# Loading the first weight in partition halves over two queues, with a new instruction order, in a fused FFT filter and GELU MLP kernel

## The chip, the cores and the metric

The kernel runs on one core of a Trainium2 chip. The metric is device time in microseconds (us) of one execution. The profile is one execution taken by the hardware profiler; its span is the time between its first and last instruction. Five engines run their own instruction streams and wait for each other by semaphores: PE (matmuls), VectorE (DVE), ScalarE (ACT), GpSimd (POOL) and SyncE (SP). A DMA can be issued from the queue of SyncE, ScalarE or GpSimd.

## The reference

```
xn  = layernorm(x)                       # x: 2048 x 640, bf16, no scale or shift
A   = irfft2(rfft2(xn) * (w_r + 1j*w_i)) # filter over both axes; w: 2048 x 321
B   = gelu(xn @ w1 + b1) @ w2 + b2       # w1: 640 x 1536, w2: 1536 x 640, tanh gelu
out = x + A + B                          # bf16
```

## The kernel before

The 2048 rows are cut into 16 chunks of 128 rows (chunk c holds rows 16p + c). All work is written as operations of a small scheduler class; each has a number in the order of its creation. The string `ORDER` lists all numbers, each with the letter of its engine (s, p, a, d, g) and its buffer slots, and so fixes the order on every engine by hand; `sync` only adds the waits. The times written at the loads (`at`) and the durations in the operations were for choosing the order: they do not reach the program.

*Loads.* SyncE's queue issues the chunks 0 and 1 of x singly (called x0 and x1 here, 160 KB each), then the five row blocks of W1 (block j holds rows 128j to 128j+127, 128 partitions x 3072 bytes, 384 KB each), then chunks 2 and 3 of x in one transfer (here x2, 320 KB), the table G (gtab, 512 KB), the other chunks in pairs, the bias b2, W2 in three parts (640 KB each), smaller tables, the filter weights (Wf, transfers of 16 partitions with runs of 642 bytes), and later a few more. ScalarE's queue issues one load, b1 (3 KB). `load` keeps the loads of one queue in their order.

*Layer norm, per chunk.* DVE computes statistics (`bn_stats`, two halves, line 478; `bn_aggr`, line 480). For chunk 0 ScalarE takes the square root (line 484) and DVE the reciprocal; then ScalarE loads the table for gelu (line 485). For the other chunks DVE adds eps (line 488) and GpSimd raises to -0.5 (line 489). DVE writes the normalised chunk (line 507).

*Transposes.* xnT holds the chunks with columns on partitions. Chunks 0 to 5 are transposed by PE (line 525) and copied by DVE and ScalarE (lines 394, 395); chunks 6 to 15 by DMA (line 516).

*Forward transform.* For a pair of chunks DVE folds the normalised rows (line 537, two operations, and line 541, four), the "T operations" of the pair; PE multiplies with gtab (ten matmuls a pair), and the result is copied to XV. When all eight pairs are there, PE goes on with etab, mtab and ntab (the filter and its way back), SyncE transposes the results by DMA, and PE ends with getab and htab.

*MLP.* The first layer of chunks 0 and 1 is made of 60 steps of two 128-wide matmuls: for each of six pairs of 128 hidden columns (b), chunk (t) and W1 block (j) one step, number 241 + 12b + 5t + j. A step waits for its block of W1, and the five blocks of one sum are taken in order. The remaining chunks follow in blocks of two and then four chunks (256 and 512 wide), gelu with bias b1col on ScalarE (lines 581, 599). The second layer (W2 times gT) fills PE between the steps of the transform; for some chunks it is done early and kept (line 759).

Before the first real work PE runs 47 matmuls on zeros (`warm`). All matmuls but the transposes have line 383, a helper.

Of the kernel before, what the change touches and what calls it, by code (L numbers as in the profile page):

```python
# [9 lines left out]
ACT = mybir.ActivationFunctionType  # L10
# [4 lines left out]
F = 1536  # L15
# [3 lines left out]
NFC = 12  # L19
# [277 lines left out]
def bass_parallel_sum__spectral_gfnet__dense_activation_gelu__prompt_kernel(  # L297
# [15 lines left out]
    w1v = B_w1.rearrange("(c p) f -> p c f", p=128)  # L313
# [5 lines left out]
    with ExitStack() as es:  # L319
# [131 lines left out]
        for ri, wsrc in enumerate((A_w_r, A_w_i)):  # L451
            for half in range(4):
# [4 lines left out]
                else:  # L457
# [14 lines left out]
        for c0, n in [(0, 1), (1, 1)] + [(c, 2) for c in range(2, 16, 2)]:  # L472
            pr = 100 - c0 / 2
            B_mv, B_ve, B_r = Buf("mv"), Buf("ve"), Buf("r")
            for c in range(c0, c0 + n):
                B_st = Buf("st")
                for h in range(2):
                    st_ops.append(K.op([("dve", 0.393)], pr, lambda e, _, c=c, h=h: e.bn_stats(stats[:, c, 6 * h:6 * h + 6], view(X, c * D + H2 * h, [[1, H2]])),  # L478
                         reads=[B_x[c]], writes=[B_st], hard=[first] if len(st_ops) == 2 else []))
# [12 lines left out]
        for pair in range(8):  # L492
            xn, x1, xf = Buf(f"xn{pair}", p_xn), Buf(f"xe{pair}", p_x1), Buf(f"xf{pair}", p_xf)

# [8 lines left out]
            for n in range(2):  # L503
# [15 lines left out]
                for j0, j1, engs in ((0, 3, ["dve"]), (3, 5, ["act"])) if c < 2 else ((0, 5, ["dve", "act"]),):  # L519
# [8 lines left out]
                    if j0 and not c:  # L528
# [280 lines left out]
```

## Time and profile before

| | us |
|---|---|
| median of 3 runs (151.99 to 152.57) | 152.36 |
| the profiled execution | 152.23 |
| its span | 150.4 |
| PE busy | 144.0 (96%) |
| DVE busy | 108.0 (72%) |
| ScalarE busy | 75.9 (50%) |
| GpSimd busy | 22.0 (15%) |

The granted clock of TensorE was 1.0 in all slices. Matmuls are pipelined and their ends are modelled, so a line's length covers a little of its neighbour; the start times and the idle times in front are what to go by. "SPq" and "ACTq" are the queues' own issuing instructions.

### The profile page before, as it was taken

How to read it: one execution, taken by the hardware profiler on the slowest of the kernel's cores; microseconds unless marked ns; L12 is line 12 of the kernel's file. 1: busy time of each engine (PE TensorE's matmuls, PEld its weight loads, DVE VectorE, ACT ScalarE, POOL GpSimd, SP SyncE). 2: the span in 40 equal slices, each digit the busy share in tenths (PEclk: the TensorE clock that was granted, in tenths of full speed). 3: DMA queues.
4: the chain of work that ended last, by engine and by line, in shares of the span. 5: the costliest groups of instructions: out<-in, count | busy, mean ns of one | idle time of the engine just before them, and what ended most of it. 6: DMA issues, size and time to landing. Idle time of an engine off the chain costs nothing.

```text
span 150.4 us, 4033 instructions
## 1 busy us (share of the span) xinstructions
PE 144.0 (96%) x1726; PEld 90.4 (60%) x1726; DVE 108.0 (72%) x236; ACT 75.9 (50%) x124; POOL 22.0 (15%) x35
## 2 busy tenths in 40 slices
PE   7779999999989999999999999999999999999993
PEld 7669997565555645445545545445666565665662
DVE  2739999989973559775989989720499859666622
ACT  3514994566978768788594552141765040042000
POOL 2102031112400012000000000000000292380330
PEclk9999999999999999999999999999999999999999
DMA  4999997889778928702620621896000366679093
GB/s 133 308 383 404 348 395 141 150 127 111 141 159 150 191 27 251 275 1 57 124 57 10 127 48 31 104 221 124 17 0 0 44 82 97 87 132 209 12 127 93
DMA packets 28499, 20.68 MB, mean 137 GB/s; under 512 B 18881, under 2 KB 25793, under 8 KB 28482
## 3 DMA queue, kind: packets, MB, share of 16 engines
q1 hardware_dynamic: 25888, 15.51, 42.9%
q0 software_dynamic: 2592, 4.92, 16.8%
q8 instruction: 13, 0.21, 0.6%
q14 instruction: 4, 0.03, 0.1%
q10 hardware_dynamic: 2, 0.00, 0.0%
HBM read 13.54 MB, written 5.24 MB: 125 GB/s over the span
## 4 chain that ended last, share of the span: by engine, by line
PE 80%; DMA 10%; DVE 6%; SPq 1%; issue 1%; ACT 1%; ACTq 0%
PE ps L383 79%; DMA W<-in_B_w_dram 4%; DMA xnT<-T 3%; DMA XV<-T 2%; DVE T L541 1%; DVE stats L478 1%; SPq L375 1%; PE ps L525 1%; DVE T L537 1%; DVE T L507 1%; DVE T L395 1%; DVE X L759 1%; ACT T L394 1%; SPq L691 0%; DVE mv L480 0%
## 5 line engine op out<-in xcount | busy, mean ns | idle before, releaser
L383 PE MATMUL ps<-xnT,W 128*128 128x512 bf16 (+2 forms) x360 | 58.4, 309 | 2.5 <-DMA W<-in_B_w_dram 1.9
L383 PE MATMUL ps<-W,gT 128*128 128x512 bf16 (+3 forms) x396 | 58.1, 295 | 0.0
L383 PEld LDWEIGHTS ps<-W,gT 128*128 128x128 bf16 x396 | 30.2, 98 | 22.9 <-issue 2.2
L383 PEld LDWEIGHTS ps<-xnT,W 128*128 128x128 bf16 x360 | 31.8, 114 | 19.8 <-DMA W<-in_B_w_dram 2.2
L599 ACT ACTIVATE gT<-ps,b1col 128x512 bf16<-128x512 f32 (+1 forms) x48 | 29.0, 637 | 10.6 <-PE ps L383 10.5
L775 POOL DMA_DIRECT2D out_dram<-W x14 | 12.6, 1079 | 74.0 <-DVE W L768 74.0
L394 ACT ACTIVATE Wf<-ps 128x960 bf16<-128x960 f32 (+1 forms) x10 | 8.2, 862 | 17.4 <-PE ps L383 17.4
L478 DVE BATCH_NORM_STATS2 stats<-X 128x6 f32<-128x320 bf16 x32 | 14.1, 478 | 2.1 <-DMA X<-in_A_x_dram 2.1
L666 DVE TENSOR_TENSOR T<-Y,Wf 128x1288 bf16<-128x1288 bf16 x16 | 12.6, 820 | 0.0
L394 ACT ACTIVATE XV<-ps 128x1280 bf16<-128x1280 f32 (+2 forms) x9 | 9.9, 1118 | 4.2 <-PE ps L383 4.2
L489 POOL TENSOR_TENSOR rstd<-ve,mhalf 128x2 f32<-128x2 f32 (+1 forms) x8 | 6.5, 814 | 31.6 <-DVE ve L488 31.6
L395 DVE CAST Xb<-ps 128x960 bf16<-128x960 f32 (+1 forms) x5 | 5.9, 1181 | 6.1 <-PE ps L383 6.1
L394 ACT ACTIVATE Xb<-ps 128x960 bf16<-128x960 f32 (+1 forms) x7 | 7.6, 1108 | 4.9 <-PE ps L383 4.9
L722 DVE TENSOR_TENSOR Wf<-Wf 128x960 bf16<-128x960 bf16 (+1 forms) x12 | 6.8, 599 | 2.8 <-ACT Wf L394 2.6
L394 ACT ACTIVATE T<-ps 128x512 bf16<-128x512 f32 (+1 forms) x12 | 4.6, 437 | 8.0 <-DMA XV<-T 5.2
L541 DVE TENSOR_TENSOR T<-T 128x512 bf16<-128x512 bf16 (+1 forms) x32 | 8.6, 315 | 0.1
L395 DVE CAST Y<-ps 128x644 bf16<-128x644 f32 x7 | 5.8, 828 | 3.7 <-PE ps L383 3.6
L768 DVE TENSOR_TENSOR W<-ps,b2bc 128x640 bf16<-128x640 f32 x6 | 4.9, 821 | 4.8 <-PE ps L383 4.8
L507 DVE TENSOR_SCALAR T<-X,mv,rstd 128x640 bf16<-128x640 bf16 x16 | 6.8, 438 | 1.7 <-issue 1.0
L394 ACT ACTIVATE Y<-ps 128x644 bf16<-128x644 f32 x9 | 6.3, 709 | 3.5 <-PE ps L383 3.5
L759 DVE TENSOR_TENSOR X<-ps,b2bc 128x640 f32<-128x640 f32 x7 | 5.7, 819 | 3.2 <-PE ps L383 3.2
L383 PE MATMUL ps<-getab,XV 32*128 32x160 bf16 (+1 forms) x128 | 7.5, 242 | 0.0
(52 smaller groups left out, 127.0 us busy)
## 6 DMA issues: line engine op xcount, KB each, us to landing
out_dram<-in_A_x_dram POOLq DMA_DIRECT2D x4, 640.0 KB, 7.1
X<-in_A_x_dram SPq DMA_DIRECT2D x7, 320.0 KB, 8.1
out_dram<-W POOLq DMA_DIRECT2D x14, 160.0 KB, 4.2
W<-in_B_w_dram SPq DMA_DIRECT2D x5, 384.0 KB, 6.6
W<-in_B_w_dram SPq DMA_DIRECT2D x3, 640.0 KB, 12.6
Wf<-in_A_w_r_dram SPq DMA_DIRECT2D x7, 160.5 KB, 3.9
Wf<-in_A_w_i_dram SPq DMA_DIRECT2D x7, 160.5 KB, 3.4
gtab<-c_G SPq DMA_DIRECT2D x1, 512.0 KB, 7.9
```

The source lines that it names most:

```text
L383: ins = e.matmul(o_, lhsT=lw, rhs=rh, start=st, stop=sp_, skip_group_check=True)
L394: return e.activation(dst(), src(), ACT.Copy, scale=scale)
L395: return e.tensor_copy(dst(), src())
L478: st_ops.append(K.op([("dve", 0.393)], pr, lambda e, _, c=c, h=h: e.bn_stats(stats[:, c, 6 * h:6 * h + 6], view(X, c * D + H2 * h, [[1, H2 ...
L489: K.op([("pool", 0.75)], 400 + pr, lambda e, _, a=a, b=b: e.tensor_tensor(out=rstd[:, a:b], in0=ve[:, a:b], in1=mhalf[:, a:b], op=ALU.pow) ...
L507: o = K.op([("dve", 0.356)], pr, lambda e, _, c=c, n=n, xnv=xnv: e.tensor_scalar(out=xnv(n, 0, [[1, D]]), in0=view(X, c * D, [[1, D]]), sc ...
L541: ring_ops.append(K.op([("dve", 0.333 if w == 128 else 0.136)], pr, lambda e, _, op=op, x1v=x1v, xfv=xfv, o_=o_, o0=o0, o1=o1, w=w: e.tens ...
L599: K.op([("act", act_us(128 * nt, 1) + 0.02)], pr + PRIO["gelu"], lambda e, _, c0=c0, nt=nt, fc=fc, hps=hps: e.activation(gT[:, fc, 128 * c ...
L666: filt_ops.append(K.op([("dve", 0.738)], pr, lambda e, _, k=k, Y=Y, TB=TB, pair=pair: e.tensor_tensor(out=view(TT, TB.slot * 8 * KP + k * ...
L722: K.op([("dve", 0.068 + n / 6)], pr + 2, lambda e, _, k=k, op=op, yo=yo, y2=y2, n=n: e.tensor_tensor(out=view(Wf, Y2 + y2.slot * 3 * D + ( ...
L759: kept_ops.append(K.op([("dve", 0.735)], 30, lambda e, _, kps=kps, xo=xo: e.tensor_tensor(out=xo, in0=psb(kps.slot, [[1, D]]), in1=b2bc[:] ...
L775: last.append(K.op([("pool", 0.9)], 450, lambda e, _, c=c, os_=os_: e.dma_start(ov[:, c, :], view(W1, OST + os_.slot * D, [[1, D]]), accum ...
```

## The change

Each block of W1 is loaded as two transfers of 64 partitions x 3072 bytes (192 KB): partitions 0 to 63 from ScalarE's queue, partitions 64 to 127 from SyncE's. The two halves share one semaphore. ScalarE's first half waits for the identity matrix that GpSimd makes (so that it is issued behind it); the other four follow it. x2 is issued behind the third half on SyncE, ahead of blocks 3 and 4. The operations get new numbers, five more from there on: a first-layer step is now 246 + 12b + 5t + j, the transposes of chunks 1, 2 and 3 are 133 and 135, 147, and 150, and the T operations of the first pair are 139 to 142.

The order on all engines is new. On PE, all six steps with block 0 now stand in front of the first with block 1, and 50 of the 60 steps in front of the transposes of chunks 2 and 3 (before, 54 steps and the gtab matmuls of pair 0); 8 of the 47 warm matmuls stand behind the first transposes, and the b1 matmuls ahead of them. On DVE, the four T operations of pair 0 now stand behind the statistics of chunks 2 and 3 instead of in front. On ScalarE, the gelu table load stands directly behind the square root instead of behind the first xnT copy. On GpSimd the identity comes first.

`hard` entries only hold the order search to a sequence on one engine (the table load in front of the copies, GpSimd's powers behind the loads queued there); they add no wait.

```diff
 ORDER = """
-9s 2a 1d 7g 0d 4g 8p:4 3g 11a 10s 6g 12s 13s 14s 15s 55d 54d 16s 17s 56d 60d 57a 18s 59d 121d:1 19s 125p:3 61d 20s 122p:1 124p:4 52p:3 62d 21s 123d 126a 63d 58a 22s 64g 301p:7
-277p:4 302p 23s 289p:2 253p:0 278p 265p:1 24s 127d 279p 290p 291p 53a 266p 25s 241p:6 133d:0 128p:5 130p:3 303p 26s 129d 242p 131a 254p 267p 132d 280p 27s 268p 282p 283p 134d:1
-284p 28s 285p 243p 136d 258p 281p 29s 304p 135d 286p 137d 294p 306p 30s 287a 244p 305p 270p 65d 307p 288a 31s 255p 295p 68d 292p 308p 32s 296p 309p 69d 297p 310p 66d 33s 139p:3 70d
+9s 2a 0d 3g 8p:7 11a 10s 4g 5g 12a 13s 14a 15s 16a 17s 19a 18s 60d 21a 59d 20s 1d 22s 61d 65d 62a 23s 63a 64d 126d:1 57p:2 24s 66d 25s 129p:1 127p:6 67d 26s 130p:0 131a 68d 128d
+69g 58a 27s 246p:6 258p:7 270p:5 28s 282p:4 294p:0 306p:1 132d 271p 29s 307p 283p 259p 138d:0 133p:2 30s 135p:3 295p 134d 247p 31s 136a 296p 284p 137d 248p 260p 32s 311p 74d 263p
+299p 251p 33s 252p 70d 275p 312p 272p 71d 34s 264p 287p 300p 301p 73d 35s 265p 308p 302p 72d 309p 75d 36s 266p 261p 76d 276p 142d:1 277p 77g 141d 288p 273p 297p 139d 278p 262p 267p
...
 """
...
-        for j, at in enumerate((4.6, 5.75, 6.9, 8.05, 9.2)):
-            load(W1[:, F * j:F * j + F], w1v[:, j, :], B_w1s[j], 393216, prio=next(pr), at=at)
-        load_x(2, 2, next(pr), at=10.1)
-        load(gtab[:], const["G"], B_g, 524288, prio=next(pr), at=11.4)
+        for j, at in enumerate((5.4, 6.4, 7.5, 9.5, 10.6)):
+            if j == 3:
+                load_x(2, 2, next(pr), at=8.4)
+            for q, p0 in (("act", 0), ("sp", 64)):
+                load(part(W1, p0, 64, F * j, [[1, F]]), w1v[p0:p0 + 64, j, :], B_w1s[j], 196608, q=q, prio=next(pr) if q == "sp" else 408 - j, at=at, reads=[] if q == "sp" else [B_id], group=f"w1_{j}")
+        load(gtab[:], const["G"], B_g, 524288, prio=next(pr), at=11.8)
...
-        K.op([("act", 0.2)], 200, lambda e, _: e.activation(b1col[:], psb(B_b1ps.slot, [[1, NFC]]), ACT.Copy), reads=[B_b1ps], writes=[B_b1c])
+        tob1 = K.op([("act", 0.2)], 200, lambda e, _: e.activation(b1col[:], psb(B_b1ps.slot, [[1, NFC]]), ACT.Copy), reads=[B_b1ps], writes=[B_b1c])
...
-                K.op([("act", 1.3)], 410, lambda e, _: e.preload_act_table(ACT.Gelu_apprx_tanh), reads=[B_ve], writes=[Buf("table2")])
+                table2 = K.op([("act", 1.3)], 410, lambda e, _: e.preload_act_table(ACT.Gelu_apprx_tanh), reads=[B_ve], writes=[Buf("table2")])
...
-                 reads=[B_ve, B_mh], writes=[B_r] + B_rs[a:b])
-
+                 reads=[B_ve, B_mh], writes=[B_r] + B_rs[a:b], hard=list(queued["pool"]))
+
+        tob1.hard.append(table2)
...
-                         reads=[tps], writes=[B_xnT[c]])
+                         reads=[tps], writes=[B_xnT[c]], hard=[table2] if not c and engs == ["act"] else [])
```

More of the change, by code (lines that the diff above doesn't have):

```diff
@@ L257 @@
-138p 67d 34s 246p 71d 269p 140a 256p 74d 72g 259p 271p 260p 77d 257p 261p 298p 272p 5g 247p 141d:0 293p 311a 273p 144d 142p:5 73d 145p:4 143a 262p 245p 146d 248p 274p 312a 249p
-250p 84d 325p:4 252a 90d 337p:5 276a 331p:7 82d 251a 326p 76d 332p 300a 340p:3 147d:0 275a 338p 148d 346p:6 299a 85d 347p 327a 343p:1 81d 348a 313p:2 75d 83d 314p 333a 78d 86d 341p
-101d 339a 322p:6 87d 263a 323p 98d 328p:7 315a 79d 97d 587p:4 80g 342a 108d 319p:2 264a 151d:0 88g 344p 324a 156d:0 329p 320p 150d 330a 588p 152d 159d 149d 316p:3 89d 317p 589p
@@ L260 @@
-171d:1 318a 173d 590p 321a 99d 176d:0 174s 334p:6 175d 157p:2 335p 93d 591p 336a 91d 172s 180d:1 92d 592p 158a 117d 604p:6 345a 105d 605p 35s 100d 178d 606p 177d 36s 179d 160p:0
-94d 37s 607p 114d 161a 95d 593d 608p 38s 96g 609p 162d:0 154p:0 610d 153p 181p:3 155a 182p 186d:1 349p:6 102d 184d 163d 373p:7 185s 183a 109d 350p 165d:1 103d 164d 374p 104g 166d
-39s 382p:4 167d 375a 106d 187s 168p:1 116d 351a 379p:5 189d:0 188d 380p 197d:0 169p 113d 358p:7 198s 170a 118d 193d:1 190d 352p:6 115d 110d 119d 199d 383p 40s 381a 120g 191d 192d
@@ L263 @@
-359p 384a 200s 107d 353p 202d:0 111d 194p:0 201d 112g 354a 195p 225d:1 361p:5 41s 196a 203d:0 205d 355p:4 42s 204d 206d 223d 356p 360a 228d:0 224s 362p 227d 207p:1 363a 210d:0 208p
-394p:6 232d:0 43s 209a 230d 231d 397p:5 212d 211s 229d 395p 357a 215d:0 234p:1 396a 233p 214d 44s 391p:7 218d:0 236a 213s 219d 392p 217d 216d 235a 400p:6 393a 221p:0 45s 220p 398p
-46s 222a 406p:4 226s 407p 399a 457p:0,0 47s 385p:5 458d 459a 48s 386p 49s 747d 460p:0,1 387a 408a 401p 462d 461a 367p:5 368p 478p:0 439p:4 479d:0 480a:1 440p 402a 475p:0 237g
@@ L269 @@
-527a 624p 450a 533d:0 513p:0 625p 514a:2 515d:1 626p 530d:1 516p:0 627p 517d 518a 640p:4 757d 521s 628p 472p:0,1 534d 522s 529d 641p 473a 642p 532d:0 474a 519s 643p 629d 644p 531d
-547p:0 520s 535d:1 645p 549d:1 548a:0 659p:6 536d 550p:0 660p 552d 551a 661p 553d:1 537p:0 662p 557d:0 539a:1 663p 646d 538a:2 664p 554d 540p:0 676p:4 541a 542d 677p 665d 546s 678p
-679p 558d 680p 545s 556d:0 681p 559d:1 555d 695p:6 560d 543s 696p 682d 697p 51s 561p:0 544s 712p:4 562d:0 563a:1 698p 564p:0 699p 565a 713p 566a 568s 700p 454p:0 701d 567s 714p
@@ L272 @@
-433p:7 715p 570s 434p 716p 435a 569s 442p:6 443p 427p:7 455p 428p 456a 717p 429a 669p:0 718d 444a 451p:6 670d:0 671a 421p:4 422p 673d:0 597p:0 672d 423a 675d:0 452p 598d:1 599a
-436p:7 453a 437p 674d 571p:0 438a 600d:0 614p:4 601d 572a:0 578p:6 602d:1 573a 579p 603d 580p 575d:0 683p:0 630p:2 684d:7 615p 616p 574d 685g 631d:0 611p:0 617p 612d:2 581p 702p:2
-618p 703d:5 619p 704g 620p 633p:0 621d:4 632g 577d:1 650p:4 576d 634a:1 622g 651p 635a 582p 613g 583p 637d:0 652p 636d 594p:2 584p 595d:7 653p 654p 585d:1 655p 639d:1 586g 686p:6
@@ new lines @@
+69g 58a 27s 246p:6 258p:7 270p:5 28s 282p:4 294p:0 306p:1 132d 271p 29s 307p 283p 259p 138d:0 133p:2 30s 135p:3 295p 134d 247p 31s 136a 296p 284p 137d 248p 260p 32s 311p 74d 263p
+299p 251p 33s 252p 70d 275p 312p 272p 71d 34s 264p 287p 300p 301p 73d 35s 265p 308p 302p 72d 309p 75d 36s 266p 261p 76d 276p 142d:1 277p 77g 141d 288p 273p 297p 139d 278p 262p 267p
+140d 289p 7g 290p 146d:0 269a 285p 286p 37s 249p 149d 291p 268a 250p 253p 147p:2 293a 38s 150p:7 79d 292a 279p 274p 148d 298p 151a 310p 313p 303p 153d:0 314p 315p 281a 254p 152d
@@ new lines @@
+255p 345p:7 316a 81d 333p:4 280a 334p 87d 317a 346p 78d 351p:5 335a 352p 156d:0 257a 143p:1 80d 82d 144p 347a 342p:4 90d 256a 343p 157d 321p:7 353a 155d 83d 336p:6 89d 344a 322p
+154d 145a 337p 86d 348p:5 324p:4 84d 98d 85g 349p 323a 113d 325p 158p:1 338a 88d 91d 159p 161d:0 326a 330p:7 164d 160a 327p:6 92d 121d 331p 93g 339p:4 122d 340p 114d 328p 332a
+165p:3 123d 350a 176d:1 162p:2 341a 318p:7 97d 177s 319p 329a 111d 592p:4 320a 167d:0 593p 305a 168d 39s 304a 110d 609p:6 166a 112d 610p 170d:0 178d 163a 611p 99d 94d 179s 95d 594p
@@ new lines @@
+115d 169d 595p 172d 40s 116d 119d 612p 117g 96d 41s 171d 613p 180d:0 173p:0 42s 105d 614p 215d:0 596p 615d 216s 597p 181d 174p 100d 360p:7 598d 101g 43s 361p 217d 6g 357p:4 103d
+218s 362a 185d:1 189d:1 358p 175a 191d 372p:5 106d 190s 182d 387p:7 359a 183d 184d 373p 193d:0 192s 186p:0 194d 187p 354p:4 118d 188a 196d:1 197d 44s 355p 198d 120d 388p 195d 45s
+356a 124d 369p:6 219d:0 125g 389a 107d 102d 370p 220d 374a 200p:1 199p 104d 228d:0 363p:4 201a 108d 230d 109g 384p:5 223d:0 231s 222d 224d 221d 378p:7 371a 204d:1 226p:0 202d 229s
@@ new lines @@
+225p 207d:0 364p 227a 206d 379p 209d:1 46s 375p:6 211d 208d 365a 210d 47s 376p 233d:0 380a 385p 48s 232d 212p:0 386a 213p 205s 234d:0 432p:7 237d 214a 236d 441p:5 235d 49s 433p
+377a 238p:0 203s 239p 426p:4 240d 241a 442p 50s 462p:0,0 443a 51s 453p:6 52s 464d 463a 427p 53s 465p:0,1 428a 54s 414p:5 467a 466d 415p 454p 434a 752d 480p:0 417p:4 481d:0 482a:1
+418p 416a 483p:0 390p:7 484a 485d 242g 391p 487d:0 468p:0,0 392a 243g 486d 419a 408p:7 490d:1 469a 244g 411p:4 491d 245g 470a 412p 489d:1 409p 488d 402p:5 493d:0 413a 492d 403p
@@ new lines @@
+455a 504p:0 423p:4 506a:0 505d:1 424p 404a 494p:0 425a 393p:5 495d:2 496a:1 429p:6 410a 497p:0 430p 499d 498a 450p:4 431a 502s 507p:0 394p 508d 509a 399p:6 503s 515d:1 471p:0,0
+514d 501s 396p:7 472d 473a 451p 55s 400p 395a 510d:0 500s 474p:0,1 452a 517d:0 456p:4 476d 475a 397p 444p:5 511d 398a 528p:0 513d:1 457p 530a:1 512d 459p:7 516d 529a:0 460p 458a
+518p:0 401a 445p 519d:1 405p:4 520a:2 406p 446a 531p:0 420p:6 532d 533a 421p 461a 538d:1 521p:0 422a 447p:7 539d 407a 435p:6 522d 523a 438p:5 535d:0 524s 477p:0,0 534d 439p 527s
@@ new lines @@
+478a 479d 448p 436p 440a 541d:1 552p:0 526s 536d:0 437a 366p:5 553d:1 554a:0 367p 525s 537d 449a 555p:0 540d 381p:4 556d 557a 645p:6 368a 563d:1 542p:0 382p 544d:0 543a:2 646p 383a
+559d:0 647p 545p:0 562d 648p 547a 558d 649p 546a 550s 628p:4 561d:0 564d:1 629p 560d 650p 551s 565d 630p 651d 631p 56s 632p 548s 681p:6 566p:0 549s 633p 568d:0 567a:1 682p 634d
+569p:0 683p 571d 570a 664p:4 575s 665p 684p 685p 572s 666p 686p 574s 667p 687d 668p 573s 669p 717p:6 670d 718p 762d 719p 720p 721p 722p 583p:4 723d 638p:0 700p:6 639d:1 640a 701p
@@ new lines @@
+584p 641d:0 576p:0 642d 585p 577a:0 578d 702p 644d:0 703p 643d 602p:0 580d:0 579d 704p 603a:1 604d 586p 705p 581d:1 674p:0 706d 582d 587p 676d:0 675a 619p:6 588p 606d:0 589p 599p:2
+590d:0 620p 671p:0 605d 655p:4 600d:4 656p 621p 672d:2 601g 652p:2 657p 653d:3 658p 608d:1 654g 659p 607d 622p 591g 660p 678d:0 661p 677d 616p:0 635p:2 662d:6 623p 617d:5 624p 625p
+636d:7 727p:4 618g 728p 680d:0 663g 710p:0 626d:4 637g 691p:6 712a:1 711d 673g 692p 693p 679d 627g 694p 713d:0 707p:2 714d 695p 696p 708d:3 697p 729p 709g 698d:5 730p 716d:1 699g
@@ L278 @@
+736p:6 715d 731p 737p 688p:0 732p 689d:0 733p 738p 734d:2 739p 735g 724p:2 763p:4 725d:7 764p 740p 726g 741p 742p 765p 690g 743d:1 745p:0 744g 753p:6 747a:1 754p 746a 766p 755p
+748d:0 749d 772p:5 756p 750d:0 767p 751d 768p 757p 769p 758p 770d:4 759p 771s 773p 774p 760d:3 775p 776p 777p 781p:4 778p 782p 783p 761s 779d 784p 785p 786p 780s 787p 788d 789s
 """
```

6 lines of the change are left out of this document (removed).

## The prediction

> **What bounds the kernel now.** The page first: PE is busy for 144.0 of 150.4 us, so the time is PE's fixed work plus PE's gaps. The table of slices gives PE, VectorE and the DMA engines:
>
> ```profile
> PE   7779999999989999999999999999999999999993
> ...
> DVE  2739999989973559775989989720499859666622
> ...
> DMA  4999997889778928702620621896000366679093
> ```
>
> PE has one weak place, the first three slices (0 to 11 us); DVE is full from 11 to 41 us. PE's own timeline shows the gaps (start, length, engine, what, idle before it):
>
> ```profile
> 5.27 0.45 PE L525 MATMUL ps<-ident,T 128*128 128x128 bf16 x5
> 5.65 0.56 PE L383 MATMUL ps<-ident,gT 1*128 1x1 bf16 x12
> 6.20 0.41 PE L383 MATMUL ps<-xnT,W 128*128 128x128 bf16 x4
> 8.34 0.75 PE L383 MATMUL ps<-xnT,W 128*128 128x128 bf16 x10 [1.73 <-DMA W<-in_B_w_dram]
> 9.29 0.75 PE L383 MATMUL ps<-xnT,W 128*128 128x128 bf16 x10 [0.20 <-DMA W<-in_B_w_dram]
> ...
> 42.72 1.92 PE L383 MATMUL ps<-xnT,W 128*128 128x512 bf16 x8 [0.55 <-DMA xnT<-T]
> ...
> 98.16 0.52 PE L383 MATMUL ps<-Z,ntab 32*32 32x320 bf16 x32 [0.30 <-ACT T L394]
> ```
>
> After the first transposes PE stands still for 1.73 + 0.20 + 0.55 + 0.30 = 2.78 us. That is all that an earlier start and a better order can win. DVE's timeline shows the partner that limits PE from 12 us on:
>
> ```profile
> 11.04 1.03 DVE L541 TENSOR_TENSOR T<-T 128x512 bf16<-128x512 bf16 x4
> 12.05 1.67 DVE L478 BATCH_NORM_STATS2 stats<-X 128x6 f32<-128x320 bf16 x4
> ...
> 42.75 0.45 DVE L507 TENSOR_SCALAR T<-X,mv,rstd 128x640 bf16<-128x640 bf16 x1 [0.96 <-issue]
> ...
> 45.46 1.03 DVE L541 TENSOR_TENSOR T<-T 128x512 bf16<-128x512 bf16 x4
> ```
>
> DVE works almost without a gap from the landing of x2 (chunks 2 and 3) to the last T operation at 46.49 us. The gtab matmuls of the last pair stand on PE at 46.85, only 0.36 later.
>
> Last the DMA issues, one at a time (KB, us from issue to landing), and then the table by microsecond (last two columns: DMA share, GB/s):
>
> ```profile
> W<-in_B_w_dram SPq DMA_DIRECT2D x1, 384.0 KB, 4.0
> W<-in_B_w_dram SPq DMA_DIRECT2D x1, 384.0 KB, 6.2
> X<-in_A_x_dram SPq DMA_DIRECT2D x1, 320.0 KB, 8.0
> gtab<-c_G SPq DMA_DIRECT2D x1, 512.0 KB, 7.9
> ```
>
> ```profile
> 6.00:7.00 1.00, 0.61 (x11) 0.38 (x8) 0.31 (x3) 0.98 (x2) 0.57 (x1) 1.00 0.80 227
> 7.00:8.00 1.00, 0.00 (x0) 0.00 (x0) 0.76 (x2) 0.62 (x2) 0.00 (x0) 1.00 0.88 267
> ```
>
> With the issue times (W1 blocks 0 and 1 at 1.65 and 2.12, x2 at 4.02, gtab at 5.41) the landings are 5.65, 8.32, 12.02 and 13.31. From block 1 to x2 are 1472 KB in 3.70 us, to gtab 512 KB in 1.29: 398 KB per us both times. So behind the dip at 6 to 8 us a transfer lands at 12.02 - (2560 - C) / 398, where C is the KB that the engines have moved up to its end.
>
> **The change, part by part.** *Issues.* A DMA issue takes 0.43 to 0.50 us. SyncE keeps the halves of partitions 64 to 127 and all other loads, with x2 ahead of blocks 3 and 4. ScalarE gets five issues of about 0.47 behind the identity, from about 1.4 to 3.8; its Sqrt waits for DVE's mean until 4.21 in any case, so they cost nothing; were that cover gone, the first chunk would be late by the excess.
>
> *Bytes.* Nothing is saved; the two rings share the 16 engines, which are already busy (shares 0.8 to 1.03). By bytes: when x2 lands, SyncE's ring has moved x0, x1, three halves and x2 (1216 KB) and ScalarE's all five halves (960): C = 2176 against 2560, so x2 lands at 11.06, 0.96 earlier. Block 1 needs 704 KB of SyncE's ring, while ScalarE's, which has no x0 and x1 ahead of it, runs ahead; C is 1088 if it is served strictly in order of issue (8.32) and 704 + 704 if the rings share evenly (9.13). I take 9.13, for nothing holds ScalarE's ring back. Block 2 then is due by C = 1792 at 10.1, block 3 by 2368 at 11.5, block 4 by 2560 at 12.0.
>
> *PE's new order.* A first-layer step is two matmuls: 58 in 3.29 us, 0.113 a step. Before, two steps ran before block 1 was needed; now all six steps of block 0 do (246, 258, 270, 282, 294, 306): from 6.25 to 6.93. Then PE waits for block 1: 9.13 - 6.93 = 2.20 us. Behind it come 6 steps and the five transposes of chunk 1 (0.28), so block 2 is wanted at 10.1; 18 more to the first use of block 3, at 12.1; 10 more to block 4, at 13.3: no further wait. After 44 steps in all (4.99 + 0.28) PE wants chunk 2's transposes (147) at 14.40.
>
> *x2's chain.* From x2's landing to these transposes the trace has 15.59 - 12.02 = 3.57. The new order puts four T operations (1.03) where two statistics (0.89) bridged GpSimd's power: about 0.08 more. 11.06 + 3.65 = 14.71, so PE waits 0.31 more. Early gaps: 2.20 + 0.31 = 2.51 against 1.93.
>
> *DVE.* The list of its work up to the last T operation has the same instructions. Before, the four T operations of pair 0 filled the time before x2; now they come behind it. End of the chain: 46.49 - 0.96 + 1.03 = 46.56. The earlier x2 is used up by that. On PE five matmuls of 512 (0.217 each) stand between the last gtab matmuls and the first etab ones where seven stood, so 0.43 more work lies ahead of the former, and PE comes there at 46.85 + 0.43 + (2.51 - 1.93) = 47.86, or 47.31 without the wait of 0.55. DVE is ready at 46.56; the 0.55 at 42.2 may go, and the 0.30 at 98 I keep.
>
> *Table load and b1col.* The load (1.28) moves from 6.16 to between Sqrt and the xnT copy: 4.53 to 5.81, the copy then starts at 5.83 instead of 5.76: 0.07, inside the 6.25 above. b1col is wanted first by the gelu at 12.03. GpSimd's reordered memsets hide likewise.
>
> *Sum at full rate.* Gaps 2.51 + 0.30 + (0 to 0.55) against 2.78: 0.03 to 0.58 more, 0.3 in the middle: 152.23 + 0.3 = 152.5. (152.23 is the profiled execution, span 150.4 plus 1.8 around it, 0.1 under the median.)
>
> *What a half costs.* No row shows a transfer to 64 partitions. The nearest rows: whole blocks at 398 KB per us, and the Wf loads to 16 partitions each, four of them together at 150 to 232 GB/s:
>
> ```profile
> 29.50:30.50 1.00, 1.00 (x9) 0.55 (x8) 0.89 (x2) 0.35 (x1) 0.54 (x1) 1.00 1.08 232
> ...
> 31.50:32.50 1.00, 1.00 (x11) 0.65 (x9) 1.00 (x5) 1.00 (x2) 0.00 (x0) 1.00 1.15 150
> ```
>
> The eight halves that pass before x2 are 1536 KB: 3.86 us at 398, 8.4 at 184, the middle of the Wf rows. So the price lies between 0 and 4.5 us, and goes one for one into x2 and PE (147 waits for it). The halves keep 3072-byte rows like whole blocks, unlike Wf's 642; I take a fifth of the way: 0.9. **Forecast: 152.5 + 0.9 = 153.4 us, slower.**
>
> A rule speaks against the change here. The Trainium skill, "SBUF — State Buffer", section "Door 1: The DMA port swizzle", says that 64 neighbouring partitions reach only half of the 16 DMA ports. By it two halves in flight on both rings pair up, but of ScalarE's five, two run beside x0, x1 and x2 without a partner, and each would take 0.96 instead of 0.48: also about 0.96 on x2. No run here shows it yet.
>
> **Rivals.** (1) *The dip goes: faster.* Blocks 0 and 1 land 2.67 apart, later ones 0.96 on average by the rate. The 1.7 us lost there fall together with 227 and 267 GB/s. If a second ring keeps the engines fed, block 1 comes at 7.4, x2 at 9.4, and the early gaps fall to about 0.8: 152.5 - 1.7 = 150.8. It decides once x2 lands before about 10.2 (0.9 under 152.5 is the lower edge of no change). For it: the engines' share was under 0.9 there, so something besides bytes held them. Against: the share was still 0.8, with slow packets rather than an empty queue, and the one ring was not short of work (its eighth issue, at 4.02, was held for 1.35 us).
>
> (2) *The rings only share: no change*, 152.5, as summed without a price. The Trainium skill, "DMA: Bandwidth & Descriptors", section "Rules for kernel authors", says of two transfers to disjoint partition halves that one should not bother, as they serialize on the same engines; that is this case.
>
> (3) *The new order stalls behind 15 us: slower still.* At pair 2's gtab matmuls PE arrives about 0.4 after DVE; in the old trace DVE lost 1.35 us (0.39 for PE, 0.96 at 41.8). If it loses them before pair 2, PE waits about 1: 154.4 on top of the forecast.
>
> **Chances.** Forecast 0.40 (its own range 152.9 to 154.2), dip gone 0.30, only sharing 0.20, stalls 0.10. A measurement here tells about 0.5%, 0.76 us: faster is below 151.6, slower above 153.1. Rival 1 gives faster 0.30; sharing, with a little of the forecast's low end, same 0.24; the rest slower 0.46. The range from 150.4 to 154.8 leaves the far end of the stalls and the best of rival 1.
>
> **What would show it.** In the changed profile: PE's wait for W behind its first twelve W1 matmuls near 2.2 to 3.1 us (right) or under 0.6 (rival 1); x2's landing at 12 (price), 11 (sharing) or under 10.2; 227 and 267 GB/s at 6 to 8 us gone or not; PE idle at L528 for chunk 2; the last T operation near 47.5. I am wrong if block 1 lands before 8 us, or if PE's idle from 15 us on differs by over 1 us from 0.85.

## The result, and the profile after

| | before | after |
|---|---|---|
| median of 20 runs each, us | 152.29 | 152.84 |
| lowest to highest, us | 150.87 to 153.83 | 152.09 to 153.80 |
| the profiled execution, us | 152.23 | 152.77 |
| its span, us | 150.4 | 151.0 |

The ratio is 1.0049 (95% interval 1.0027 to 1.0071): the changed kernel is slower by 0.5 us in the medians. The granted clock was 1.0 in both profiled executions. A ratio leaves out executions more than 1.5% above the fastest of the same kernel; of the kernels below this touches one, the order alone, where it leaves out four of twelve.

The table of slices of the changed kernel, PE, DVE and the DMA engines:

```profile
PE   7975999999999999999999999999999999999993
...
DVE  2736999999987478848867999545399999895363
...
DMA  5999998789746993968700441697000028796852
```

PE's weak slices are now 1, 3 and 4 (to 15 us) instead of 1 to 3. DVE's fourth slice (11.3 to 15.1 us) is a 6 where it was a 9, and its full stretch begins later. PE's timeline (start, length, engine, what, idle before it and what ended it) says what PE waits for:

```profile
6.83 0.83 PE L383 MATMUL ps<-xnT,W 128*128 128x128 bf16 x12 [0.22 <-DVE xnT L395]
8.19 0.64 PE L383 MATMUL ps<-xnT,W 128*128 128x128 bf16 x8 [0.53 <-DMA W<-in_B_w_dram]
...
9.87 2.20 PE L383 MATMUL ps<-xnT,W 128*128 128x128 bf16 x36 [0.54 <-DMA W<-in_B_w_dram]
13.62 2.42 PE L383 MATMUL ps<-xnT,W 128*128 128x128 bf16 x40 [1.55 <-DMA W<-in_B_w_dram]
16.30 0.89 PE L528 MATMUL ps<-ident,T 128*128 128x128 bf16 x10 [0.26 <-DVE T L510]
```

Blocks 1, 2 and 3 of W1 are each waited for, 2.62 us together; with the two waits for DVE the gaps are 3.10 us, where the kernel before had 2.78. The two later gaps of the kernel before (0.55 at 42 us, 0.30 at 98 us) are gone. (From 90 us on the timeline has five more gaps of 0.16 that wait for nothing. They stand where records of matmuls are missing, 383 of 396 in that group, and are not counted.) The first W1 matmul starts at 6.83 instead of 6.20; 0.22 of that is the gap in its line, 0.41 stands ahead of it. So 3.10 - 2.78 + 0.41 = 0.73 explains the 0.6 of the span within the small overlaps of such lines.

The table by stretches of the changed kernel (stretch, length, busy PE, PEld, DVE, ACT, POOL, granted clock, DMA share, GB/s) shows why the blocks are late:

```profile
5.00:6.00 1.00, 1.00 (x22) 0.83 (x20) 0.96 (x3) 1.00 (x1) 0.00 (x0) 1.00 0.87 258
...
8.00:9.00 1.00, 0.81 (x14) 0.81 (x15) 0.12 (x1) 0.00 (x0) 0.00 (x0) 1.00 1.07 257
...
10.00:12.00 2.00, 2.00 (x36) 1.91 (x35) 0.00 (x0) 0.00 (x0) 0.00 (x0) 1.00 1.08 253
```

From 3 to 12 us the engines move 243 to 261 GB/s in every stretch, with a share of about 1: they are busy, but with slow packets. Whole blocks had 398 KB (of 1024 bytes) per us, which is 408 GB/s. The landings follow, by the list of DMA issues (KB, us from issue to landing):

```profile
X<-in_A_x_dram SPq DMA_DIRECT2D x1, 320.0 KB, 8.9
W<-in_B_w_dram SPq DMA_DIRECT2D x1, 192.0 KB, 9.3
```

The first is x2, issued at 3.65 and landed at about 12.6. The second is SyncE's half of block 3, issued at 4.28 behind x2 and landed at 13.6: PE's wait of 1.55. ScalarE's and DVE's timelines:

```profile
1.49 3.10 ACTq L375 DMA_DIRECT2D W<-in_B_w_dram  x5
4.64 0.30 ACT L486 ACTIVATE ve<-mv,eps 128x1 f32<-128x1 f32 x1 [2.63 <-DVE mv L482]
```

```profile
12.62 1.67 DVE L480 BATCH_NORM_STATS2 stats<-X 128x6 f32<-128x320 bf16 x4 [2.83 <-DMA X<-in_A_x_dram]
...
47.02 1.03 DVE L544 TENSOR_TENSOR T<-T 128x512 bf16<-128x512 bf16 x4
```

ScalarE's five issues took 3.10 (0.62 each) and pushed the square root from 4.24 to 4.64. DVE stands idle for 2.83 before x2, since the T operations that filled this time now stand behind it; its last T operation ends at 48.05, 1.56 later than before. PE's last early wait, 0.26 for chunk 2's transposes at 16.30, ends 3.68 behind x2's landing at 12.62. x2 therefore decides when PE goes on: had block 3 come earlier, PE would have waited longer here.

### The profile page after: what moved, and what is told of

The parts are those of the page before. It is cut to its first block, busy times and chain, and to the rows that moved or that the text cites. A ratio compares the mean times of both kernels' runs of the same rounds, so it can differ in the third digit from the quotient of the medians.

```text
span 151.0 us, 4033 instructions
## 1 busy us (share of the span) xinstructions
PE 143.3 (95%) x1713; PEld 90.8 (60%) x1726; DVE 112.7 (75%) x242; ACT 71.4 (47%) x118; POOL 22.4 (15%) x35
## 4 chain that ended last, share of the span: by engine, by line
PE 86%; DMA 6%; DVE 2%; SPq 2%; issue 1%; POOL 1%; ACT 0%
PE ps L383 85%; DMA X<-in_A_x_dram 6%; SPq L375 2%; DVE stats L480 1%; PE ps L528 1%; POOL rstd L491 1%; ACT Y L394 0%; DVE T L510 0%; DVE W L771 0%; DVE mv L482 0%; DVE ve L490 0%
## 5 line engine op out<-in xcount | busy, mean ns | idle before, releaser
L383 PE MATMUL ps<-W,gT 128*128 128x128 bf16 (+3 forms) x383 | 54.5, 292 | 1.2 <-issue 0.8
L394 ACT ACTIVATE Wf<-ps 128x960 bf16<-128x960 f32 (+1 forms) x7 | 5.9, 855 | 37.9 <-PE ps L383 37.9
L394 ACT ACTIVATE XV<-ps 128x1280 bf16<-128x1280 f32 (+1 forms) x8 | 9.5, 1185 | 2.4 <-PE ps L383 2.3
L544 DVE TENSOR_TENSOR T<-T 128x128 bf16<-128x128 bf16 (+1 forms) x32 | 8.5, 311 | 0.1
L584 ACT ACTIVATE gT<-ps,b1col 128x256 bf16<-128x256 f32 x12 | 5.0, 483 | 5.7 <-PE ps L383 5.7
L540 DVE TENSOR_TENSOR T<-T 128x640 bf16<-128x640 bf16 x16 | 7.4, 485 | 0.2
```

The source lines that it names most:

```text
L383: ins = e.matmul(o_, lhsT=lw, rhs=rh, start=st, stop=sp_, skip_group_check=True)
L394: return e.activation(dst(), src(), ACT.Copy, scale=scale)
L544: ring_ops.append(K.op([("dve", 0.333 if w == 128 else 0.136)], pr, lambda e, _, op=op, x1v=x1v, xfv=xfv, o_=o_, o0=o0, o1=o1, w=w: e.tens ...
```

## The experiments

All are told as ratio to the kernel before in the same batch; medians of 6 to 12 executions. "Halves" are the two transfers of a block, "whole" is one transfer of 128 partitions.

**Whole blocks with the new order.** The loop over the two queues is replaced; the order is the changed one with the numbers of the missing halves taken out.

```diff
-            for q, p0 in (("act", 0), ("sp", 64)):
-                load(part(W1, p0, 64, F * j, [[1, F]]), w1v[p0:p0 + 64, j, :], B_w1s[j], 196608, q=q, prio=next(pr) if q == "sp" else 408 - j, at=at, reads=[] if q == "sp" else [B_id], group=f"w1_{j}")
+            load(W1[:, F * j:F * j + F], w1v[:, j, :], B_w1s[j], 393216, prio=next(pr), at=at)
```

> The new order with whole W1 blocks of 128 partitions on SyncE's queue alone, x2 still behind the third. Theory (64 neighbouring partitions a transfer keep the engines at 255 GB/s where whole blocks reach 398): the rate is back at 380 to 410 GB/s from 8 us on, block 1 lands at 8.3, x2 at 10.1, block 4 at 12.0; PE's early waits fall from 3.1 to about 1.5 us, the Sqrt no longer waits for ScalarE's issues (0.4); time about 151.1. Rival A (two queues at once are slow, whatever the partitions): the same here. Rival B (the new order itself is what costs): time stays at 152.3 or above.

Measured 149.60, ratio 0.9829 (0.9801 to 0.9858): faster than the forecast for it, and 3.2 us under the changed kernel. The stretches of this kernel:

```profile
5.00:6.00 1.00, 1.00 (x19) 0.79 (x17) 0.93 (x4) 0.82 (x1) 0.00 (x0) 1.00 1.02 402
...
8.00:9.00 1.00, 1.00 (x22) 1.00 (x20) 0.56 (x2) 0.38 (x1) 0.00 (x0) 1.00 1.03 410
```

The same share of the engines now carries 402 and 410 GB/s. Block 1 landed at about 7.0, x2 at 9.12, and PE's only gap behind its start is 0.61. So the new order and x2's place together are a gain, and loading in these halves takes it back.

**Two queues kept, other halves.** ScalarE loads the even partitions, SyncE the odd ones: 64 partitions, 192 KB and rows of 3072 bytes as in the change.

```diff
+    w1a = B_w1.rearrange("(c p r) f -> p c r f", p=64, r=2)
...
-            for q, p0 in (("act", 0), ("sp", 64)):
-                load(part(W1, p0, 64, F * j, [[1, F]]), w1v[p0:p0 + 64, j, :], B_w1s[j], 196608, q=q, prio=next(pr) if q == "sp" else 408 - j, at=at, reads=[] if q == "sp" else [B_id], group=f"w1_{j}")
+            for q, p0 in (("act", 0), ("sp", 1)):
+                load(bass.AP(tensor=W1, offset=p0 * 5 * F + F * j, ap=[[2 * 5 * F, 64], [1, F]]), w1a[:, j, p0, :], B_w1s[j], 196608, q=q, prio=next(pr) if q == "sp" else 408 - j, at=at, reads=[] if q == "sp" else [B_id], group=f"w1_{j}")
```

> As the changed kernel, but ScalarE's queue loads the even partitions of each block and SyncE's the odd ones: the same sizes, rows, queues and places, only other 64 partitions. Theory: the rate is 370 to 400 GB/s, x2 lands near 11.1, block 3 near 11.6, PE's early waits fall to about 2.2, time about 152.0. Rival A (two queues): 255 GB/s and x2 at 12.6 as in the changed kernel, 152.8. Rival B (order): 152.8.

Measured 150.66, ratio 0.9891 (0.9864 to 0.9919): 1.3 under the 152.0 expected, and well under both rivals. Its stretches, PE's timeline and DVE's start on x2:

```profile
5.00:10.00 5.00, 4.60 (x79) 4.09 (x77) 3.34 (x10) 2.12 (x4) 0.57 (x1) 1.00 1.00 336
8.00:9.00 1.00, 1.00 (x20) 1.00 (x20) 0.42 (x2) 0.16 (x1) 0.00 (x0) 1.00 0.93 333
```

```profile
6.92 1.60 PE L384 MATMUL ps<-xnT,W 128*128 128x128 bf16 x20 [0.27 <-DMA W<-in_B_w_dram]
...
14.26 0.89 PE L529 MATMUL ps<-ident,T 128*128 128x128 bf16 x10 [0.73 <-DVE T L511]
```

```profile
10.57 1.67 DVE L481 BATCH_NORM_STATS2 stats<-X 128x6 f32<-128x320 bf16 x4 [1.09 <-DMA X<-in_A_x_dram]
```

Only which 64 partitions a half has is changed, and the mean rate from 5 to 10 us is 336 GB/s instead of 255. This kernel is the changed one without the price of neighbouring halves: gaps of 1.00, x2 at 10.57. Two queues, 64 partitions and 192 KB alone cost less: 1.1 us against whole blocks (149.60), whose mean rate was 393. ScalarE's issues were as slow here (3.13, the square root at 4.68). Every second partition is also every second row of W1 in memory, and the runs do not part the two. But whole blocks read neighbouring rows as well, at 393.

**Halves by columns.** Each queue loads 128 partitions x 768 columns.

```diff
-            for q, p0 in (("act", 0), ("sp", 64)):
-                load(part(W1, p0, 64, F * j, [[1, F]]), w1v[p0:p0 + 64, j, :], B_w1s[j], 196608, q=q, prio=next(pr) if q == "sp" else 408 - j, at=at, reads=[] if q == "sp" else [B_id], group=f"w1_{j}")
+            for q, f0 in (("act", 0), ("sp", F // 2)):
+                load(W1[:, F * j + f0:F * j + f0 + F // 2], w1v[:, j, f0:f0 + F // 2], B_w1s[j], 196608, q=q, prio=next(pr) if q == "sp" else 408 - j, at=at, reads=[] if q == "sp" else [B_id], group=f"w1_{j}")
```

> As the changed kernel, but each block is halved by columns: all 128 partitions, 768 columns (1536 bytes a row) on ScalarE's queue and 768 on SyncE's. Theory (it is the 64 neighbouring partitions): full rate, 350 to 400 GB/s from 8 us on, x2 near 11, time within 0.5 of the kernel with every second partition, 150.7. Rival (a ring that carries half of a block, or short rows, is slow): 255 GB/s and 152.8.

Measured 150.23, ratio 0.9877 (0.9839 to 0.9916), as expected, with a mean of 382 GB/s from 5 to 10 us and x2 at 9.58:

```profile
8.00:9.00 1.00, 1.00 (x22) 1.00 (x20) 0.76 (x2) 0.38 (x1) 0.00 (x0) 1.00 1.05 390
...
10.00:12.00 2.00, 1.76 (x32) 1.61 (x30) 1.97 (x9) 0.00 (x0) 0.22 (x1) 1.00 1.03 401
```

Here ScalarE's five issues took 2.53 and the square root stood at 4.19, not delayed.

**Halves on one queue.** Both halves of each block go to SyncE, first partitions 0 to 63, then 64 to 127; x2 stands behind the sixth half.

```diff
-            for q, p0 in (("act", 0), ("sp", 64)):
-                load(part(W1, p0, 64, F * j, [[1, F]]), w1v[p0:p0 + 64, j, :], B_w1s[j], 196608, q=q, prio=next(pr) if q == "sp" else 408 - j, at=at, reads=[] if q == "sp" else [B_id], group=f"w1_{j}")
+            for q, p0 in (("sp", 0), ("sp", 64)):
+                load(part(W1, p0, 64, F * j, [[1, F]]), w1v[p0:p0 + 64, j, :], B_w1s[j], 196608, q=q, prio=next(pr), at=at, group=f"w1_{j}")
```

> The new order with both halves of each block (partitions 0 to 63, then 64 to 127) one after the other on SyncE's queue, none on ScalarE's. Theory: a half alone is slow too, 200 to 255 GB/s while W1 is moved; block 1 lands near 8, x2 near 10.5 to 11, block 4 near 14; time about 152. Rival A (two queues): one queue is fast, 380 to 410 GB/s, landings as with whole blocks (x2 10.1, block 4 12.0), about 151.1. Rival B (order): 152.3 or above with either rate.

Measured 153.97, ratio 1.0127 (1.0084 to 1.0170). The rate is as slow as in the change:

```profile
5.00:6.00 1.00, 0.80 (x17) 0.72 (x14) 0.93 (x5) 0.99 (x2) 0.00 (x0) 1.00 1.02 243
...
10.00:12.00 2.00, 1.43 (x26) 1.27 (x24) 1.77 (x6) 0.00 (x0) 0.00 (x0) 1.00 1.04 241
```

With the two runs of other halves this shows what the price hangs on: the neighbouring partitions, not the second queue. The rate was expected rightly, the time 2 us too low: PE's gaps are spread over seven places (0.20, 0.20, 0.29, 0.41, 0.57, 0.42 and 1.22, the last behind a gelu at 17.8), which the sum by x2 alone did not see. DVE also waited 2.57 us for chunks 4 and 5 (at 16.78), which stand behind all ten halves here.

**The halves alone.** The kernel before with the two-queue loop, x2 behind the fifth block as before, and its own order with the numbers shifted by the five added loads.

```diff
-            load(W1[:, F * j:F * j + F], w1v[:, j, :], B_w1s[j], 393216, prio=next(pr), at=at)
+            for q, p0 in (("act", 0), ("sp", 64)):
+                load(part(W1, p0, 64, F * j, [[1, F]]), w1v[p0:p0 + 64, j, :], B_w1s[j], 196608, q=q, prio=next(pr) if q == "sp" else 408 - j, at=at, reads=[] if q == "sp" else [B_id], group=f"w1_{j}")
```

> The kernel before, order and place of x2 (behind the fifth block) included, with each W1 block halved over the two queues as in the changed kernel. Theory: 255 GB/s until W1 is in, block 1 near 8, x2 near 13.5 to 14, DVE's chain 1.5 later, time 153.5 to 154. Rival A: the same. Rival B (order): as before, 152.3.

Measured 153.33, ratio 1.0079 (1.0046 to 1.0113), a little under the forecast:

```profile
5.00:6.00 1.00, 1.00 (x12) 1.00 (x10) 0.95 (x3) 0.00 (x0) 0.00 (x0) 1.00 1.01 255
```

The rate came as expected, but x2 landed at 12.46 and not at 13.5 to 14. The halves cost the old order 1.2 us (0.0079 x 152.3). They cost the new one more, 0.0220 x 152.3 = 3.4 against whole blocks: there x2 moved from about 9.1 to 12.62, here from between 11.3 and 12.02 (three profiles) to 12.46.

**Order alone and x2's place alone.** First the kernel with whole blocks and the new order, with x2 moved back behind the fifth block:

```diff
         for j, at in enumerate((5.4, 6.4, 7.5, 9.5, 10.6)):
-            if j == 3:
-                load_x(2, 2, next(pr), at=8.4)
             load(W1[:, F * j:F * j + F], w1v[:, j, :], B_w1s[j], 393216, prio=next(pr), at=at)
+        load_x(2, 2, next(pr), at=10.1)
```

> The new order with the loads of the kernel before: whole blocks on SyncE's queue, x2 behind the fifth. It parts the order from x2's place. If the gain of whole blocks with x2 behind the third (149.6) is x2's place: x2 lands 2 us later, near 11.3 to 12, PE waits for chunk 2's transposes until 15 to 15.6, about 151.0 to 151.6. If it is the order alone: 149.6 to 150.0. If block 1 again lands at 8.3, behind a dip at 6 to 8 us as in the kernel before, PE waits 1.4 for it.

Then the kernel before, with nothing changed but x2 moved ahead (and the numbers in `ORDER` that this shifts):

```diff
         for j, at in enumerate((4.6, 5.75, 6.9, 8.05, 9.2)):
+            if j == 3:
+                load_x(2, 2, next(pr), at=8.4)
             load(W1[:, F * j:F * j + F], w1v[:, j, :], B_w1s[j], 393216, prio=next(pr), at=at)
-        load_x(2, 2, next(pr), at=10.1)
```

> The order of the kernel before, whole blocks, x2 behind the third. If x2's place alone gives the gain: about 150. If, as the trace says, the old order wants x2 only behind the T operations of pair 0 (DVE at 12.05) and PE's wait for block 1 comes first: 151.8 to 152.3, the waits for W1 as before or longer for blocks 3 and 4.

The order alone gave 152.88 as the median of twelve, and a ratio of 0.9978 (0.9931 to 1.0026) over eight of them. Both mix two groups: five executions at a granted clock of 1.0 with 150.88 to 151.19 (median 150.94, 0.992 of the kernel before) and seven at 0.989 with 152.79 to 153.59 (median 153.17, 1.007). The expected time is that of the first group. PE's timeline and the stretches of a profile of the second group:

```profile
14.69 0.88 PE L522 MATMUL ps<-ident,T 128*128 128x128 bf16 x10 [1.97 <-DVE T L504]
15.41 4.57 PE L379 MATMUL ps<-xnT,W 128*128 128x128 bf16 x35
```

```profile
16.00:18.00 2.00, 2.00 (x18) 1.73 (x16) 2.00 (x6) 1.88 (x5) 0.00 (x0) 0.51 1.02 392
18.00:20.00 2.00, 2.00 (x16) 1.56 (x14) 2.00 (x10) 1.08 (x3) 0.00 (x0) 0.64 1.01 410
```

PE waits 1.97 us for chunk 2, as x2 (landed at 11.01) is late for this order. From 16 to 20 us its clock is at about half, which loses 0.98 + 0.72 = 1.70 us of work (2.00 x 0.49 and 2.00 x 0.36). x2's place alone gave 152.64, ratio 1.0026 (0.9994 to 1.0058): no gain, and a little above what was expected. Neither part alone brings what both together do (0.9829), not even the order at its full clock (0.992).

**The gap filled.** The kernel with the order alone, and 24 matmuls on zeros (1.5 us) on PE, which the order places in front of chunk 2's transposes.

```diff
+        idle(24, 24 * mm_us(128))
```

> The new order with the loads of the kernel before, and 24 matmuls on zeros (1.4 us) in front of the transposes of chunk 2, where PE stood still for 1.97 us. Without them the executions fell in two groups: 150.9 to 151.2 with a mean granted clock of 1.0, 152.8 to 153.6 with 0.989 (half the clock for 3.4 us behind the gap). Theory (the gap itself brings the half clock): all executions at 1.0 and near 151.0. Rival (the half clock comes of something else, a matter of the run): two groups as before.

Measured 151.49, ratio 0.9940 (0.9914 to 0.9965), 0.5 above the expected time, with all executions at a clock of 0.999 to 1.0. The gap of 1.97 is now 0.67:

```profile
15.21 0.88 PE L522 MATMUL ps<-ident,T 128*128 128x128 bf16 x10 [0.67 <-DVE T L504]
```

With the gap filled the second group is gone (none of twelve, against seven of twelve), so it came with the gap and not with the order as such. How long the gap was in the five executions at full clock is not known, as none of them was profiled. Clocks of 0.987 to 0.989 also occur elsewhere: in two of the 23 executions of the kernel before in one batch, and in three of ten with the halves alone.

**x4 ahead of gtab.** Whole blocks, new order, and chunks 4 and 5 loaded in front of gtab, because in the first experiment DVE waited 1.28 us for them at 14.39.

```diff
-        load(gtab[:], const["G"], B_g, 524288, prio=next(pr), at=11.8)
         for c in range(4, 16, 2):
             load_x(c, 2, next(pr))
+            if c == 4:
+                load(gtab[:], const["G"], B_g, 524288, prio=next(pr), at=11.8)
```

> The kernel with whole blocks and x2 behind the third, with chunks 4 and 5 (x4) loaded ahead of gtab. There DVE waited 1.28 us for x4 and PE 0.61 behind it. Theory (the waits at the start go one for one into the end): x4 lands 1.3 earlier, PE's 0.61 goes, gtab 0.8 later is still early (its first use is at 17.05): 149.0. Rival (PE is then bound by DVE's chain, which is as long as before): 149.6.

Measured 149.32, ratio 0.9822 (0.9779 to 0.9864). PE's gap of 0.61 is gone, but the time lies between theory (149.0) and rival (149.6) and is not to be told apart from the first experiment's. Which of the two holds stays open.

**Both kernels again.** Two more executions of the kernel before and one of the changed kernel. Is block 1's landing at 8.32 a property of the kernel before, or of its one profiled execution?

> The kernel before once more, for its landings. Theory (the dip at 6 to 8 us and block 1's late landing at 8.3 are a matter of the single execution): block 1 lands between 7.0 and 8.3 and PE's waits for W1 and the time follow it. Rival (they belong to five whole blocks in a row on one queue): block 1 at 8.2 to 8.4, waits of 1.9 again.

> The same again: by the theory another landing of block 1 between 7.0 and 8.3; by the rival 8.2 to 8.4.

> The changed kernel once more. By the theory of the halves: 250 to 260 GB/s from 5 to 12 us again, x2 near 12.6, PE's early waits 2.5 to 3.3 us with the longest for block 3. By the rival that this too is a matter of the single execution: another rate, 300 or more.

The two executions of the kernel before took 152.86 and 151.77, with block 1 at about 7.4 and at 7.77, as the theory had it. In the second, PE's wait for it is 1.19 instead of 1.73:

```profile
7.77 0.75 PE L383 MATMUL ps<-xnT,W 128*128 128x128 bf16 x10 [1.19 <-DMA W<-in_B_w_dram]
```

In the first the warm matmuls took 5.20 instead of 4.16, so PE came later, found block 1 there and waited 0.16 for block 2; its other gaps were 0.26, 0.36, 0.51 and 0.87. The changed kernel took 152.21, with x2 at 11.87, less waiting for W1 than expected (0.59 and 0.97, none for block 1), 0.63 for chunk 2, and again

```profile
11.87 1.68 DVE L480 BATCH_NORM_STATS2 stats<-X 128x6 f32<-128x320 bf16 x4 [2.66 <-DMA X<-in_A_x_dram]
15.56 0.88 PE L528 MATMUL ps<-ident,T 128*128 128x128 bf16 x10 [0.63 <-DVE T L510]
```

```profile
10.00:12.00 2.00, 1.53 (x28) 1.37 (x25) 0.13 (x1) 0.00 (x0) 0.00 (x0) 1.00 1.07 244
```

Landings of whole blocks vary from one execution to the next: block 1 came at 8.32 in the first profile and between 7.0 and 7.8 in the seven others that have them. The rate of neighbouring halves varies less: the mean from 3 to 12 us is 255 and 263 GB/s in the two profiles of the changed kernel, 272 with the halves alone, and 251 with both halves on one queue (x0, x1 and x2, which are whole, among them).

## Why the prediction was right, and where it was not

The forecast (153.4, slower) has the sign, and the measured median (152.84) is 0.6 under it; as a ratio to the 152.36 it was made from, 1.0068 against 1.0049. The measured time lies just under the forecast's own range (152.9 to 154.2). The mechanism held: halves of neighbouring partitions are slow, x2 comes late, and PE follows x2. That the number came so near is luck, as two terms were mis-sized against each other.

*What set the time: x2.* The forecast let the price of a half go one for one into x2 and from there into PE, and this is what the runs show. PE's wait for chunk 2's transposes ends 3.68 or 3.69 behind x2's landing in both profiles of the changed kernel and with every second partition (forecast 3.65), and behind that nothing differs much: the span less x2's landing is 138.4 (151.0 - 12.62), 138.5 (150.4 - 11.87), 138.3 (148.9 - 10.57), and 138.5 with columns (148.1 - 9.58).

*The price of a half: right in kind, too small.* Forecast 0.9 ("a fifth of the way" between 0 and 4.5). The changed kernel and the one with every second partition differ in nothing else: 152.84 - 150.66 = 2.2 us (2.4 by the ratios, 0.0158 x 152.3). Against whole blocks it is 3.2. The bytes say about the same: 255 GB/s are 249 KB per us, and 1536 KB at 249 instead of 398 are 6.17 - 3.86 = 2.3. (The prediction reads the GB/s of the Wf rows as KB per us, which makes its upper bound 4.5 instead of 4.7.) The guess was pulled to whole blocks by the 3072-byte rows; the rate was in fact nearer to the four Wf loads (150 to 232).

The rule that the prediction weighed against the change, the Trainium skill, "SBUF — State Buffer", section "Door 1: The DMA port swizzle", agrees in the direction: halves of 64 neighbouring partitions ran at 255 GB/s, and halves of every second partition, which by its table reach all 16 ports, at 336. That two halves in flight on both rings pair up was a step of the prediction; the section does not state it, and the runs speak against it: the pairs moved 255 GB/s, no more than halves on one queue, one behind the other (226 to 303 from 4 to 12 us). Why pairs do not add up is not shown by any run. The Trainium skill, "DMA: Bandwidth & Descriptors", section "Rules for kernel authors", says that two transfers to disjoint partition halves serialize and names no rate. Rival 2 read it as serializing at the old rate, at no price; the halves ran at 255 GB/s instead, and rival 2 did not come true.

*The sum at full rate: too high by 1.8.* Forecast 152.5; with every second partition 0.9891 x 152.36 = 150.7. Three steps failed. First, the landings: the working took those of one execution, block 1 at 8.32 behind the dip, for constants, and came to 9.13 for block 1 and 11.06 for x2. In the other profiles block 1 of whole blocks came up to 1.3 us earlier, and with every second partition x2 came at 10.57, 0.49 earlier than forecast. Second, PE's work: 50 first-layer steps and the transposes of chunk 1 were counted as 5.95 us (0.113 a step); in the changed kernel they took 6.59 from 6.83 to 16.04, its waits of 2.62 taken off. So 0.64 of what was booked as waiting for block 1 was work. Third, the 0.30 and half of the 0.55 that were kept at 98 and 42 us did not occur: 0.58. These are 1.7 of the 1.8. With every second partition PE waits 0.27 in front of its first W1 matmul, nothing over 0.15 for block 1, and 0.73 for chunk 2 (forecast 2.20 for block 1 and 0.31). With its own x2 at 12.0 (11.06 + 0.9) the forecast should have been near 138.4 + 12.0 + 1.8 = 152.2; x2 at 12.62 in the profiled execution hid most of this.

Rival 1 (150.8) had the right time for a kernel without the price of neighbouring halves; its reason, that a second ring keeps the engines fed, is not needed, as one ring with whole blocks did it too (149.60).

*The sign named for the wait misled.* Behind its first twelve W1 matmuls PE waited only 0.53, which the prediction had given as rival 1's sign. The waits lay at blocks 1, 2 and 3, and the step "no further wait" for blocks 2 to 4 fell. Its working put SyncE's half of block 3 at 11.5; it landed at 13.6, because it stands behind x2's 320 KB in the same ring at 255 GB/s, and x2 itself came at 12.6 (forecast 12.0; the other execution 11.87). PE needed block 3 where the working said, 18 steps behind the first of block 2. In the other execution PE took block 1 at about 7.45 (6.77 + 6 steps) without a wait, which the prediction had named as a sign that it was wrong (block 1 before 8); what decides is x2, not block 1.

*ScalarE's issues: not free, but covered.* 0.62 each instead of 0.47, and the square root 0.4 late. It moved PE's first W1 matmul by about as much, but cost nothing in the end, as PE then waited for block 1 and for x2 anyway; the cover named in the prediction (the wait till 4.21) was too short.

*What held.* DVE's chain end (forecast 46.56 + 0.9 = 47.5, measured 48.05) followed x2, with the T operations behind it as worked out. Rival 3 did not occur: from 15 us on PE's idle is 0.26, 0.59 under the 0.85 named. Rival 2 failed on the halves' rate.

## What to carry to other kernels

If a load is split over two queues, split it by columns or by every second partition; neighbouring partition halves ran at 255 GB/s, where these ran at 382 and 336 and whole blocks at 393, and cost 2.2 to 3.2 us here. Whole blocks on one queue were the fastest of all. A new order and the place of the load that it needs belong together: the order alone gave 0.992 of the time at full clock and 1.007 where the clock fell, x2's place alone 1.003, both together 0.983. Find the one landing that PE's chain waits for last; earlier waits only fill the time until then. Do not take a landing time from one execution as fixed where it decides the forecast; take a spread (here 1.3 us for block 1, 0.75 for x2 in two executions of the changed kernel) and carry it into the range.

## What the runs showed of the hardware that was not expected

In one profile the clock of TensorE fell to 0.51 and 0.64 of full speed from 16 to 20 us, behind a gap of 1.97 us on PE. Seven of 12 executions of this kernel had the same mean clock of 0.989, at a cost of about 2.2 us (medians of the two groups, 153.17 and 150.94); 24 matmuls in the gap removed it in all of 12. The Trainium skill, "TensorE: Matmul & The Clock Gate", section "Why this matters for your kernels", warns of idle gaps of more than about 3 us; here the profile shows it behind a shorter one. Not every such gap does it: in the profile of the kernel before PE waited 1.73 us at 6.6 us, and the clock stayed at 1.0. A gap that a forecast books as 2 us can so cost 4.

An issue on ScalarE's queue took 0.62 us with halves by partitions (neighbouring or every second) and 0.51 (2.53 / 5) with halves by columns. No run tells why.
